# A triangular inverse by doubling: 64x64 tiles on TensorE's diagonal, or 32x32 tiles for its first four steps

## The chip, the cores and the metric

One Trainium2 chip, one of its cores. The metric is the device time of one launch in microseconds (us). One execution is also recorded by the profiler; its times are those of the tables and profile lines below. Engines go by short names: PE is TensorE's matrix multiplication and PEld its weight load, DVE is VectorE, ACT is ScalarE, POOL is GpSimd, and SP issues the DMA transfers.

## The reference

A gated delta rule over a sequence is followed by an MLP mixer, all in fp32. Batch is 4, heads 8, sequence 768, head dimension 48. Cut to what matters:

```python
k_n = k / (norm(k) + 1e-6)
for t in range(S):                                # per batch and head, state is 48 x 48
    y[t] = q[t] @ state
    v_old = state.T @ k_n[t]
    state = state + beta[t] * outer(k_n[t], v[t] - v_old)
x = y as (B, S, H * D)                            # 768 tokens of 384
h = relu(x.T @ w_tok1) @ w_tok2                   # token mixing, 768 -> 256 -> 768
u = x + h.T
out = u + relu(u @ w_ch1) @ w_ch2                 # channel mixing, 384 -> 1536 -> 384
```

## The kernel before

The sequence is cut into chunks of 128 tokens: 6 chunks for each of 4 batches, 24 in all, each with its 8 heads side by side. Within a chunk the recurrence is solved at once. With G the strictly triangular part of the beta-weighted products of the keys, the kernel needs W, the inverse of I + G, for each head (128x128). Four generators make the program:

- `prep(t)` does what doesn't depend on the state: it norms the keys (`ksq` to `krec`, `kpad`, `kbpad`), transposes (`p_t`, L301), forms the products (`p_g`, L313) and masks them on DVE into `gm` (L317). Then it builds W.
- `recur(t)` carries the state through the chunk (`p_b` L432, `p_u` L439, `p_s` L447, `p_y` L464 and L469). It uses W as `w_t`.
- `mixer(b)` is the MLP of a batch whose six chunks are done: `p_1` (L483), `p_h` (L495), transposes (L506), `p_c` (L517), `p_o` (L529).
- `load_weights` brings in the four weight matrices and rounds them with bit operations, mostly on DVE, one on POOL (L199 to L221), during the first chunks.

W is built by doubling. It begins as the identity, minus the entries of `gm` at odd columns that couple neighbours (`off`, L333 and L338 on POOL). For block sizes s = 2, 4, 8, 16, 32, one `step` joins pairs of blocks of size s into blocks of 2s. A step is a chain over two engines:

1. DVE transposes W in 32x32 blocks into T (`flip`, L345).
2. PE multiplies `gm` with the even columns of T into `p_l` (L359). This is one burst of matmuls over all heads and all tiles on the diagonal.
3. DVE masks it into `lt` (L360).
4. PE multiplies `lt` with the odd columns of W into `p_wu` (L372), again a burst.
5. DVE subtracts that from the odd columns of W (L373), called `w_o`.

In the kernel before, every step works on tiles of R = 64: rows and columns 0 to 63, and 64 to 127, so that a burst is 8 heads times 2 tiles, 16 matmuls. An fp32 matmul is two instructions of PE in the profile, each with its weight load, so a burst shows as x32. The tiles have 64 columns for each head in `w_r`, `t_r` and `lt_buf`.

After s = 32 both 64x64 diagonal blocks of W are done (`w_6`, `t_6`, which are `w_r` and `t_r` here). A correction of T (`p_x`, L399 and L400), a product (`p_l`, L410) and a last one (`p_wu`, L415) give the 64x64 block off the diagonal. POOL copies (L404 to L406) and ACT (L411, L416) fill `w_t`.

The order of the program comes from `plan`, a heap of generators with a start time and a step in units of a chunk: prep(t) runs one unit ahead of recur(t), and mixer(b) is spread over the six chunks after its batch. The framework then orders the instructions for each engine by that priority and by readiness, and places the semaphores. So matmuls of the mixer stand between the bursts of a prep where there are any. There are none for the first six chunks, apart from the first products of the mixer (L483). The last mixer stands alone at the end.

The sizes that follow R are these lines:

```python
ident_r = folded("ident_r", ident, R)
mask_1 = folded("mask_1", mask_f, R // 2)
SMALL = [s for s in (2, 4, 8, 16, 32) if s < R]
width = (R if s < R else 64) // 2          # of masks[s]
width = R if s < R else 64                 # of lt_buf[s]
for lo in range(0, 128, R):                # off, one POOL instruction for each tile
```

Of the kernel before, what the change touches and what calls it, by code (L numbers as in the profile page):

```python
# [13 lines left out]

C = 128
DP = 64
R = 64
WP = 384


# [1 line left out]
def kernel(  # L22
# [76 lines left out]
    def folded(name, full, width):  # L99

        t = const.tile([128, width], FP32, name=name)
        nc.gpsimd.tensor_copy(out=t, in_=full[:, 0:width])
        for lo in range(width, full.shape[-1], width):
            nc.gpsimd.tensor_tensor(
                out=t, in0=t, in1=full[:, lo : lo + width], op=ALU.add
            )
        return t

    ident_r = folded("ident_r", ident, R)

# [3 lines left out]
    for sign in (1, -1):  # L114
# [3 lines left out]
        )  # L118
    mask_1 = folded("mask_1", mask_f, R // 2)

    SMALL = [s for s in (2, 4, 8, 16, 32) if s < R]
    masks = {}
    for s in (2, 4, 8, 16, 32):
# [9 lines left out]
        )  # L133
        width = (R if s < R else 64) // 2
        masks[s] = folded(f"mask_{s}", m.rearrange("p n s -> p (n s)"), width)
# [11 lines left out]
    for s in (2, 4, 8, 16, 32):  # L147
        width = R if s < R else 64
        lt_buf[s] = const.tile([128, H, width], FP32, name=f"lt_{s}")
# [112 lines left out]
    def prep(t):  # L262
# [62 lines left out]

        w_r = work.tile([128, H, R], FP32, name="w_r", bufs=1)
        t_r = work.tile([128, H, R], FP32, name="t_r", bufs=1)
# [277 lines left out]
```

## Time and profile before

| | |
|---|---|
| time, median of 3 runs | 1278.59 us (1268.81 to 1278.84) |
| the profiled execution | 1278.59 us |
| its span, first to last instruction | 1276.8 us |
| granted PE clock, mean | 0.908 |
| PE busy | 1169.6 us (92%) |
| PEld busy | 920.6 us (72%) |
| DVE busy | 431.3 us (34%) |
| POOL busy | 197.0 us (15%) |
| ACT busy | 180.7 us (14%) |
| chain that ended last | PE 86%, DVE 8%, POOL 4% |

A line of the costliest groups gives the line of the kernel, the engine and the operation, what is written and read, the size (for PE rows*columns of the tile and partitions x elements of the moving operand), the count, then busy us, mean ns of one, and the idle time of that engine just before such instructions, with what ended it. A matmul is pipelined, and its end is modelled, so its mean ns is longer than the pace at which matmuls follow each other. A line of the timeline gives start and duration in us of several merged instructions, their count, and in brackets the idle time before them. The row of PEclk gives the granted clock of PE in tenths, in 40 slices of 31.9 us.

### The profile page before, as it was taken

Reading aid. Unit: us, or ns where it says so; the run is one execution under the profiler, and the core shown is the slowest. Engines: PE = TensorE matmul, PEld = TensorE weight load, DVE = VectorE, ACT = ScalarE, POOL = GpSimd, SP = SyncE. Lnnn points to the kernel's source line nnn. Section 1 sums busy time; section 2 is a strip of 40 time slices with the busy share of each in tenths; the row PEclk is TensorE's granted clock in tenths of the full one; section 3 lists DMA queues with packets and bytes.
Section 4 is the critical chain, followed back from the end, with each engine's and each line's share of the span. In section 5 each row is a group of like instructions: output and inputs, shape, how many; then the busy total and the mean of one; then the engine's idle time right before and its main releaser. Section 6 shows DMA issues by size and latency. Waiting matters only on the chain.

```text
span 1276.8 us, 27386 instructions
## 1 busy us (share of the span) xinstructions
PE 1169.6 (92%) x12462; PEld 920.6 (72%) x12462; DVE 431.3 (34%) x898; ACT 180.7 (14%) x407; POOL 197.0 (15%) x295
## 2 busy tenths in 40 slices
PE   4788787788999999999999999999999999999998
PEld 3767676677787777777677777777677777786776
DVE  6766674332334323322322313322323322211000
ACT  2001011011111120120121120220121120111111
POOL 6233141111111110110110110110111110000000
PEclk9986575776999999899897998999799999799999
DMA  6232230010001000100000100100000000000000
GB/s 123 79 85 77 70 89 25 14 26 8 15 14 26 21 13 15 32 13 14 20 14 8 32 14 14 32 14 14 20 14 8 14 1 8 7 1 13 13 13 13
DMA packets 83395, 33.31 MB, mean 26 GB/s; under 512 B 75824, under 2 KB 78896, under 8 KB 83280
## 3 DMA queue, kind: packets, MB, share of 16 engines
q1 hardware_dynamic: 83280, 31.56, 10.2%
q8 instruction: 98, 1.61, 0.5%
q14 instruction: 17, 0.14, 0.0%
HBM read 26.84 MB, written 4.72 MB: 25 GB/s over the span
## 4 chain that ended last, share of the span: by engine, by line
PE 86%; DVE 8%; POOL 4%; issue 2%; ACT 0%; POOLq 0%; ACTq 0%
PE p_c L517 15%; PE p_o L529 15%; PE p_l L359 12%; PE p_wu L372 12%; PE p_g L313 4%; PE p_u L439 4%; PE p_y L469 4%; PE p_h L495 3%; PE p_t L301 3%; PE p_l L410 2%; PE p_wu L415 2%; PE p L483 2%; DVE t_r L345 2%; PE p_x L399 2%; POOL off L333 2%
## 5 line engine op out<-in xcount | busy, mean ns | idle before, releaser
L517 PE MATMUL p_c<-u_t,wc 128*128 128x256 f32 x864 | 227.8, 405 | 0.1
L359 PEld LDWEIGHTS p_l<-t_r,gm 64*64 64x64 f32 x3840 | 144.3, 155 | 111.4 <-issue 89.4
L359 PE MATMUL p_l<-t_r,gm 64*64 64x32 f32 x3840 | 157.3, 238 | 65.0 <-DVE t_r L345 60.0
L529 PE MATMUL p_o<-wc,r 128*128 128x384 f32 x576 | 216.8, 507 | 0.0
L372 PEld LDWEIGHTS p_wu<-w_r,lt 64*64 64x64 f32 x3840 | 146.5, 158 | 56.7 <-DVE lt L360 33.0
L517 PEld LDWEIGHTS p_c<-u_t,wc 128*128 128x128 f32 x864 | 159.7, 197 | 25.5 <-issue 2.6
L372 PE MATMUL p_wu<-w_r,lt 64*64 64x32 f32 x3840 | 160.6, 240 | 14.0 <-DVE lt L360 14.0
L529 PEld LDWEIGHTS p_o<-wc,r 128*128 128x128 f32 x576 | 101.2, 191 | 50.9 <-issue 2.9
L360 DVE TENSOR_TENSOR lt<-p_l,mask 128x256 f32<-128x256 f32 x120 | 50.9, 424 | 175.2 <-PE p_l L359 175.0
L317 DVE TENSOR_TENSOR gm<-p_g,mask_u 128x512 f32<-128x512 f32 x96 | 62.0, 685 | 129.3 <-PE p_g L313 129.2
L373 DVE TENSOR_TENSOR w_r<-w_r,p_wu 128x256 f32<-128x256 f32 x120 | 50.6, 421 | 158.8 <-PE p_wu L372 158.6
L345 DVE STREAM_TRANSPOSE t_r<-w_r 128x512 f32<-128x512 f32 x120 | 85.2, 710 | 45.6 <-POOL w_r L338 43.2
L522 ACT ACTIVATE r<-p_c 128x256 f32<-128x256 f32 x144 | 55.2, 383 | 249.6 <-PE p_c L517 249.6
L405 POOL COPY w_t<-w_r 64x512 f32<-64x512 f32 x24 | 15.0, 625 | 455.0 <-DVE w_r L373 455.0
L313 PE MATMUL p_g<-kbq_t,k_t 64*128 64x256 f32 x384 | 64.3, 423 | 3.8 <-DVE gm L317 3.2
L536 DVE TENSOR_TENSOR o_sb<-p_o,xb 128x384 f32<-128x384 f32 x24 | 13.4, 557 | 135.4 <-PE p_o L529 135.4
L313 PEld LDWEIGHTS p_g<-kbq_t,k_t 64*128 64x128 f32 x384 | 41.1, 198 | 20.3 <-DVE gm L317 6.5
L411 ACT COPY lt<-p_l 64x512 f32<-64x512 f32 x24 | 13.9, 580 | 279.6 <-PE p_l L410 279.6
L469 PE MATMUL p_y<-u,gm 128*128 128x48 f32 x384 | 52.1, 289 | 0.0
L469 PEld LDWEIGHTS p_y<-u,gm 128*128 128x128 f32 x384 | 50.0, 207 | 1.9 <-issue 1.0
L333 POOL TENSOR_TENSOR off<-gm,mask 64x256 f32<-64x256 f32 x48 | 36.0, 750 | 78.0 <-DVE gm L317 76.5
L215 POOL TENSOR_TENSOR w_f<-w_f,w_r 128x384 uint32<-128x384 uint32 (+1 forms) x34 | 33.5, 986 | 91.5 <-DVE w_f L207 77.8
(89 smaller groups left out, 1076.5 us busy)
## 6 DMA issues: line engine op xcount, KB each, us to landing
d<-in_moe_w_ch_dram SPq DMA_DIRECT2D x24, 384.0 KB, 3.2
k_raw<-in_k_dram SPq DMA_DIRECT2D x24, 192.0 KB, 2.7
qpad<-in_q_dram SPq DMA_DIRECT2D x24, 192.0 KB, 2.9
v_raw<-in_v_dram SPq DMA_DIRECT2D x24, 192.0 KB, 2.6
out_dram<-o_sb SPq DMA_DIRECT2D x24, 192.0 KB, 1.9
d<-in_moe_w_tok_dram SPq DMA_DIRECT2D x6, 256.0 KB, 3.0
d<-in_moe_w_tok_dram SPq DMA_DIRECT2D x4, 384.0 KB, 3.1
beta_sb<-in_beta_dram SPq DMA_DIRECT2D x1, 96.0 KB, 2.2
```

Source lines behind the costliest of these rows:

```text
L313: nc.tensor.matmul(p_g[par][:, jj], k_t[lo : lo + DP, j], kbq_t[lo : lo + DP, j])
L317: nc.vector.tensor_tensor(out=gm[:, 4 * g + par : 4 * g + 4 : 2], in0=p_g[par], in1=mask_u[:, None, None, :].to_broadcast([128, 2, 2, 128] ...
L333: nc.gpsimd.tensor_tensor(out=off[lo : lo + R], in0=gm[lo : lo + R, :, 0, lo + 1 : lo + R : 2], in1=mask_1[lo : lo + R, None, :].to_broadc ...
L345: nc.vector.transpose(dst.rearrange("p h n -> p (h n)"), src.rearrange("p h n -> p (h n)"))
L359: nc.tensor.matmul(p_l[r, h], gm[r, h, 0, r], t_e[r, h])
L360: nc.vector.tensor_tensor(out=lt_e, in0=halves(p_l, s), in1=halves(masks[s][:, None, :], s).to_broadcast([128, H, half // s, s]), op=ALU.mult,
L372: nc.tensor.matmul(p_w[r, h], lt[r, h], w_o[r, h])
L439: nc.tensor.matmul(p_u[:, h], w_t[:, h], rhs[:, h])
L469: nc.tensor.matmul(p_y[:, h], gm[:, h, 1], u[:, h], start=(c == 0 and h == 0), stop=(h == H - 1), skip_group_check=True,)
L517: nc.tensor.matmul(p_c, wc1[:, cb, f * 128 : (f + 1) * 128], u_t[:, cb], start=(cb == 0), stop=(cb == NCB - 1),)
L522: nc.scalar.activation(r, p_c, ACTF.Relu)
L529: nc.tensor.matmul(p_o, r2[f][:, i * C : (i + 1) * C], wc2[:, f], start=(f == 0), stop=(f == NHT - 1),)
```

## The change

The constant R becomes 32:

```diff
-R = 64
+R = 32
```

All that follows from it:

- `w_r`, `t_r`, `off`, `ident_r`, the masks and `lt_buf` of the steps s = 2 to 16 are half as wide.
- The bursts of these four steps run over four tiles of 32x32 on the diagonal: 8 heads times 4 tiles, 32 matmuls with 16 moving columns each. `step(s, R, w_r, t_r)` is called with 32.
- The loop over `lo` makes four `off` instructions on 32 partitions.
- Before s = 32 this branch, not taken at R = 64, spreads W and T to 64 columns for each head. `half_of` is 1 on the partitions of the first, or of the second, 32 of each 64 rows and 0 elsewhere, so that each 32x32 block lands in its place on the diagonal of its 64x64 tile:

```python
w_6 = work.tile([128, H, 64], FP32, name="w_6", bufs=1)
t_6 = work.tile([128, H, 64], FP32, name="t_6", bufs=1)
for i in range(2):
    c_i = slice(32 * i, 32 * i + 32)
    nc.gpsimd.tensor_scalar_mul(w_6[:, :, c_i], w_r, half_of[:, i : i + 1])
    nc.gpsimd.tensor_scalar_mul(t_6[:, :, c_i], t_r, half_of[:, i : i + 1])
```

- The step s = 32 and all after it run on `w_6` and `t_6` in 64x64 tiles as before.
- T was and is made by DVE transposes of 32x32 blocks, now of 128x256 elements instead of 128x512.

## The prediction

> **What bounds the kernel now.** I read the busy shares and the 40 slices first, then the costliest groups, then the timeline of single steps.
>
> ```profile
> PE 1169.6 (92%) x12462; PEld 920.6 (72%) x12462; DVE 431.3 (34%) x898; ACT 180.7 (14%) x407; POOL 197.0 (15%) x295
> ...
> PE   4788787788999999999999999999999999999998
> ...
> PEclk9986575776999999899897998999799999799999
> ...
> L359 PE MATMUL p_l<-t_r,gm 64*64 64x32 f32 x3840 | 157.3, 238 | 65.0 <-DVE t_r L345 60.0
> L372 PE MATMUL p_wu<-w_r,lt 64*64 64x32 f32 x3840 | 160.6, 240 | 14.0 <-DVE lt L360 14.0
> ...
> L345 DVE STREAM_TRANSPOSE t_r<-w_r 128x512 f32<-128x512 f32 x120 | 85.2, 710 | 45.6 <-POOL w_r L338 43.2
> ```
>
> From slice 11 (about 320 us) on TensorE (PE) is the bound; before that it waits more and its clock is down. The doubling steps (L359 and L372) hold 318 us of modelled matmul time, so the price of one burst of theirs decides. One step early and one late, from the timeline:
>
> ```profile
> 144.83 1.92 PE L359 MATMUL p_l<-t_r,gm 64*64 64x32 f32 x32 [1.70 <-DVE t_r L345]
> 146.78 0.42 DVE L360 TENSOR_TENSOR lt<-p_l,mask 128x256 f32<-128x256 f32 x1 [0.63 <-PE p_l L359]
> 147.26 1.92 PE L372 MATMUL p_wu<-w_r,lt 64*64 64x32 f32 x32 [0.52 <-DVE lt L360]
> 149.23 0.42 DVE L373 TENSOR_TENSOR w_r<-w_r,p_wu 128x256 f32<-128x256 f32 x1 [1.02 <-PE p_wu L372]
> 150.04 0.70 DVE L345 STREAM_TRANSPOSE t_r<-w_r 128x512 f32<-128x512 f32 x1
> 150.89 1.92 PE L359 MATMUL p_l<-t_r,gm 64*64 64x32 f32 x32 [1.70 <-DVE t_r L345]
> ...
> 365.54 1.12 PE L359 MATMUL p_l<-t_r,gm 64*64 64x32 f32 x32
> 366.60 1.13 PE L517 MATMUL p_c<-u_t,wc 128*128 128x256 f32 x4
> 367.66 1.12 PE L372 MATMUL p_wu<-w_r,lt 64*64 64x32 f32 x32
> 368.71 1.56 PE L517 MATMUL p_c<-u_t,wc 128*128 128x256 f32 x6
> ```
>
> Early, a step is one bare chain of 6.06 us, 3.84 of it two bursts at half clock. Late, the mixer's matmuls fill the gaps and PE never stops: each us taken out of a burst comes off the end.
>
> **What limits a burst.** A burst is 16 matmuls, each two instructions in fp32, so 32 weight loads and 32 matmuls. Compare a burst on both 64x64 tiles with one on a single tile (8 matmuls), and two cuts of the timeline 6 ns apart:
>
> ```profile
> 633.23 1.01 PEld L359 LDWEIGHTS p_l<-t_r,gm 64*64 64x64 f32 x32 [0.55 <-issue]
> ...
> 598.57 1.00 PEld L399 LDWEIGHTS p_x<-lt,w_r 64*64 64x64 f32 x16 [0.55 <-DVE w_r L373]
> 603.01 1.00 PEld L415 LDWEIGHTS p_wu<-w_r,lt 64*64 64x64 f32 x16 [0.54 <-issue]
> 604.96 1.86 PEld L439 LDWEIGHTS p_u<-bv,w_t 128*128 128x128 f32 x16 [0.30 <-POOL w_r L328]
> ...
> 633.23 0.25 PEld L359 LDWEIGHTS p_l<-t_r,gm 64*64 64x64 f32 x5 [0.55 <-issue]
> 633.23 0.25 PEld L359 LDWEIGHTS p_l<-t_r,gm 64*64 64x64 f32 x6 [0.55 <-issue]
> ```
>
> Twice the loads in the same time: the two tiles run side by side. The cuts at 633.340 and 633.346 us hold five and six loads: the other tile's load starts 6 ns after the first's. Within one tile the loads follow at (1.00 - 0.135)/15 = 58 ns for 64 columns, the same for 32 (L399) and 64 moving columns (L415), and at (1.86 - 0.19)/15 = 111 ns for 128 columns. So the weight load sets the pace, about 53 ns per 64 columns and 5 ns fixed; 32 columns would follow at about 31 ns.
>
> The Trainium skill agrees on this much. "TensorEngine Tiling (Array Packing)", Key Properties: tiles load and multiply in parallel (the trace agrees, 32 loads against 16 in 1.0 us), and a change of tiling mode drains the array (each burst here ends about 0.07 us after the next work has begun, and the number of changes stays). "TensorE: Matmul & The Clock Gate", LDWEIGHTS: the time goes with the columns, not the rows (58 against 111 ns). Against it stands Instruction Overhead on the first page: about 60 cycles a matmul whatever its width. The trace has two matmuls 6 ns apart on different tiles, so I take this as a floor for each tile, 25 ns at 2.4 GHz, below the 31 ns. No row shows four tiles at once.
>
> **The change part by part**, for 24 chunks. Steps s = 2 to 16 change shape, s = 32 stays.
>
> 1. PE bursts, 8 a chunk, 192 in all: 32 matmuls of 32x32 with 16 moving columns instead of 16 of 64x64 with 32, so 64 loads and 64 matmuls over four tiles, 16 rounds. At 31.4 ns a round and the same 0.19 us of entry and tail (1.12 - 16 x 0.058) the burst takes 0.69 us: 0.43 saved. At half clock a round falls from 107 to about 53 ns (64 columns at half speed), 1.95 to 1.14 us: 0.80 saved. Going by burst starts in the timeline, some 13 of the 48 bursts before 317 us ran at full clock and 35 at half; of the 144 later ones some 132 and 12. Early: 13 x 0.43 + 35 x 0.80 = 33.6. Late: 132 x 0.43 + 12 x 0.80 = 66.4.
> 2. DVE, narrower: the 128x256 product takes 421 ns and the 128x384 one (rhs) 551, so 1.0 ns an element. lt and w_o at 128 elements: about 0.29, 0.13 saved, 8 a chunk. Transpose 512 to 256: 0.71 to 0.45, 0.26 saved, four visible a chunk (the fifth goes beside part 4). 2.1 us of chain a chunk; early 6 x 2.1 = 12.7, late nothing, as mixer work covers it.
> 3. POOL, first product: off becomes four instructions on 32 partitions instead of two at 750 ns. By L104 (317 ns at 64 elements) and 750 at 256, one of 128 costs 0.46: 1.85 against 1.50, +0.35. L338 halves, 0.78 to about 0.49. Sum nearly 0, +0.2 taken; early +1.3. The narrower ident copy is hidden: POOL waits for PE before it anyway.
> 4. POOL, new: four tensor_scalar_mul spread w_r and t_r into 64 columns (w_6, t_6) between the s = 16 step and the s = 32 burst, in place of an immediate start. No row shows one; bounds are 0.43 us (a one-input copy at 1.0 ns an element, from 688 ns at 512) and 0.78 (L338, 256 strided elements). I take 0.5, 2.0 in a row, the DVE flip beside the first: wait after w_o from about 0.9 to 2.2, +1.3 a chunk (range +1.0 to +2.4). Queued behind them on POOL are only the w_t copies, which have over 20 us of idle before them. Early nothing covers it: 6 x 1.3 = 7.8. Late the gap held some 1.1 to 1.6 us of mixer work, and more can be put there because the program order is laid out by readiness; I take +0.3 a chunk, +5 (uncovered: +16).
> 5. Masks and memsets at the start: some 0.1 us each beside the first loads; nothing. No DMA and no queue of SP moves.
>
> Early: -33.6 - 12.7 + 1.3 + 7.8 = -37, of which I count -33, because weight-rounding work on DVE (0.35 to 1.0 us pieces in the same queue) takes some of the openings. Late: -66.4 + 5 = -61. The last 137 us are one mixer alone and stay. The clock may give some back: PE was granted half clock when less dense, and I add 5 (an estimate without a row). Sum -89 against the profiled execution: span 1276.8 - 89 + 1.8 outside it = 1190, and that execution is also the median of the three runs (1278.59; the lowest is 1268.81).
>
> **Rivals.**
> A, the forecast: four tiles side by side, 0.69 us a burst, about 1190; own range 1160 to 1220.
> B, issue binds a little: if the 6.5 ns seen between tiles were the price of each single instruction, a round is 8 x 6.5 = 52 ns, a burst 1.02 us. 145 x 0.1 = 15 saved at full clock, at half clock 47 x 0.8 = 38 at most, -4 from the rest and the clock: 1230 to 1270, by how the half-clock bursts are fed.
> C, the other side: twice the instructions cost twice the time, because instruction supply to PE, not the array, becomes the limit. Place: each of the 192 bursts. Price: the densest sustained rate in this trace is one load and matmul in 28.9 ns; at that rate 64 pairs take 1.85 + 0.19 = 2.04 us, +0.92 on 145 bursts, +0.15 on the 47 at half clock: +141, about 1419. At the skill's 60 cycles taken for the whole array, 25 ns a matmul: 1.79 us, +97, about 1376. It decides from a burst of about 1.2 us on, 7.9 ns an instruction, as parts 2 to 4 cancel to within 4 us. For it: nothing in the trace ever ran denser, PE had bursts of at most 64 instructions queued, now 128. Against it: at the head of a burst load, matmul, load, matmul start within 7 ns, and the period halves or doubles with the clock (58 to 107 ns), which a supply limit would not do.
> That four 32x32 tiles don't overlap fully is part of C by its price.
>
> **How the numbers follow.** A 0.50, B 0.10, C 0.40. The measurement tells about 1% (13 us) from no change. A is all faster; of B 0.07 is faster and 0.03 within 1%; of C 0.04, where supply binds only little, is within 1%, and 0.36 slower. So faster 0.57, same 0.07, slower 0.36. The range runs from A's lower end to C's upper price: 1160 to 1420.
>
> **What would show it.** Right: x32 loads become x64 at L359 with the PE burst at 0.6 to 0.75 us late, and the granted clock no worse; L345 near 450 ns; L360 and L373 near 290; four new POOL rows near 0.5 us, with PE p_l of s = 32 waiting on t_6 early. Wrong: late bursts of 1.2 us or more, in which the loads of one tile are over 75 ns apart; or bursts as short as forecast and a clock below 0.85, so that the mixer slows.

## The result, and the profile after

The changed kernel takes 1361.53 us (median of 4 runs, 1342.9 to 1376.08), the kernel before 1277.38 us beside it. The ratio is 1.0625, with a 95% interval of 1.0504 to 1.0746: 6% slower. The forecast was 1190 us. The profiled execution took 1360.47 us, its span is 1358.4 us. Executions of one kernel differ by up to 6% with the clock that they were granted; medians here are of all of them, ratios leave out those more than 1.5% above the kernel's fastest.

The bursts did nearly what was forecast. The page after, with the rows that answer to those shown of before:

```profile
PE 1191.2 (88%) x18606; PEld 909.1 (67%) x18606; DVE 372.1 (27%) x898; ACT 182.2 (13%) x407; POOL 285.3 (21%) x451
...
PEclk9967556767777989776877868799798879799999
...
L359 PE MATMUL p_l<-t_r,gm 32*32 32x16 f32 x6144 | 78.5, 188 | 53.2 <-DVE t_r L345 48.3
L391 POOL TENSOR_SCALAR w<-w_r,half_of 128x256 f32<-128x256 f32 x48 | 45.4, 956 | 302.8 <-DVE w_r L373 302.8
L372 PE MATMUL p_wu<-w_r,lt 32*32 32x16 f32 x6144 | 82.4, 190 | 25.3 <-DVE lt L360 14.8
L359 PE MATMUL p_l<-t,gm 64*64 64x32 f32 x768 | 32.7, 242 | 53.9 <-POOL t L392 53.9
```

L359 and L372 held 318 us of modelled matmul time over five steps, about 254 of it in the four that change (four fifths, an estimate by count); their 32x32 bursts now hold 161 us. But one operation that spreads W and T takes 0.92 to 0.96 us instead of the estimated 0.5, PE waits 53.9 us for T alone, and the row of the clock is full of sevens and eights after slice 10, where it had nines. One s = 16 step, the wait and what comes after it, from the timeline:

```profile
416.57 0.91 PE L529 MATMUL p_o<-wc,r 128*128 128x384 f32 x2
417.41 0.72 PE L372 MATMUL p_wu<-w_r,lt 32*32 32x16 f32 x64
...
418.65 1.82 POOL L391 TENSOR_SCALAR w<-w_r,half_of 128x256 f32<-128x256 f32 x2 [13.50 <-DVE w_r L373]
420.46 1.82 POOL L392 TENSOR_SCALAR t<-t_r,half_of 128x256 f32<-128x256 f32 x2
421.43 1.12 PE L359 MATMUL p_l<-t,gm 64*64 64x32 f32 x32 [1.56 <-POOL t L392]
...
425.51 1.65 PE L529 MATMUL p_o<-wc,r 128*128 128x384 f32 x2
427.09 1.91 PE L399 MATMUL p_x<-lt,w 64*64 64x32 f32 x16
```

The 32x32 burst of 64 matmuls takes 0.72 us, against 1.12 us for 32 matmuls on 64x64 tiles. Then four POOL operations take 3.6 us, first both of W, then both of T. The next burst starts 0.05 us after the third of them, as it reads the first 32 columns of T alone; before that PE is idle for 1.56 us. After that the same two matmuls of the mixer take 1.65 us instead of 0.91. The stretches of the trace around it show why; the columns are stretch, length, busy us and count of PE, PEld, DVE, ACT and POOL, granted clock, DMA share and GB/s:

```profile
404.50:419.80 15.30, 15.08 (x544) 9.46 (x542) 5.82 (x17) 1.40 (x4) 1.80 (x3) 1.00 0.06 14
419.80:423.00 3.20, 1.64 (x35) 1.31 (x34) 0.40 (x1) 0.00 (x0) 3.20 (x5) 0.99 0.02 5
423.00:437.00 14.00, 14.00 (x91) 9.18 (x90) 1.42 (x4) 0.58 (x1) 1.63 (x3) 0.52 0.11 29
```

In the third stretch PE is busy throughout, at half speed. The clock did not go down in the wait but 1.5 us after its end, at 422.9 us, and stayed down for 13.7 us of full PE work.

By stages, from the masked products of chunk 6 to the last product of the last W: early, up to chunk 6, 313.3 us before and 301.3 after, 12 won; late 823.6 and 916.8, 93 lost; the last mixer alone 140 in both.

### The profile page after: what moved, and what is told of

The parts are those of the page before. It is cut to its first block, busy times and chain, and to the rows that moved or that the text cites. A ratio compares the mean times of both kernels' runs of the same rounds, so it can differ in the third digit from the quotient of the medians.

```text
span 1358.4 us, 39863 instructions
## 1 busy us (share of the span) xinstructions
PE 1191.2 (88%) x18606; PEld 909.1 (67%) x18606; DVE 372.1 (27%) x898; ACT 182.2 (13%) x407; POOL 285.3 (21%) x451
## 4 chain that ended last, share of the span: by engine, by line
PE 77%; POOL 9%; DVE 9%; issue 4%; DMA 1%; ACT 1%; POOLq 0%; DVEq 0%; ACTq 0%; SPq 0%
PE p_o L529 15%; PE p_c L517 15%; PE p_wu L372 8%; PE p_l L359 7%; PE p_u L439 4%; PE p_g L313 4%; PE p_y L469 3%; PE p_t L301 3%; PE p_l L410 3%; PE p_wu L415 3%; POOL off L333 3%; PE p_h L495 3%; PE p_x L399 3%; POOL w L391 2%; PE p L483 2%
## 5 line engine op out<-in xcount | busy, mean ns | idle before, releaser
L359 PEld LDWEIGHTS p_l<-t_r,gm 32*32 32x32 f32 x6144 | 69.4, 116 | 91.7 <-issue 71.3
L359 PE MATMUL p_l<-t_r,gm 32*32 32x16 f32 x6144 | 78.5, 188 | 53.2 <-DVE t_r L345 48.3
L372 PEld LDWEIGHTS p_wu<-w_r,lt 32*32 32x32 f32 x6144 | 71.5, 119 | 62.8 <-issue 31.0
L391 POOL TENSOR_SCALAR w<-w_r,half_of 128x256 f32<-128x256 f32 x48 | 45.4, 956 | 302.8 <-DVE w_r L373 302.8
L372 PE MATMUL p_wu<-w_r,lt 32*32 32x16 f32 x6144 | 82.4, 190 | 25.3 <-DVE lt L360 14.8
L360 DVE TENSOR_TENSOR lt<-p_l,mask 128x128 f32<-128x128 f32 (+1 forms) x120 | 38.0, 316 | 198.8 <-PE p_l L359 197.9
L359 PE MATMUL p_l<-t,gm 64*64 64x32 f32 x768 | 32.7, 242 | 53.9 <-POOL t L392 53.9
L359 PEld LDWEIGHTS p_l<-t,gm 64*64 64x64 f32 x768 | 29.9, 160 | 64.7 <-POOL t L392 64.7
L313 PE MATMUL p_g<-kbq_t,k_t 64*128 64x256 f32 x384 | 68.6, 446 | 3.5 <-DVE gm L317 2.7
L345 DVE STREAM_TRANSPOSE t_r<-w_r 128x256 f32<-128x256 f32 x120 | 53.3, 444 | 53.4 <-POOL w_r L338 50.6
L333 POOL TENSOR_TENSOR off<-gm,mask 32x128 f32<-32x128 f32 x96 | 45.4, 472 | 95.1 <-DVE gm L317 90.7
L313 PEld LDWEIGHTS p_g<-kbq_t,k_t 64*128 64x128 f32 x384 | 43.1, 208 | 21.8 <-DVE gm L317 7.3
```

Source lines behind the costliest of these rows:

```text
L313: nc.tensor.matmul(p_g[par][:, jj], k_t[lo : lo + DP, j], kbq_t[lo : lo + DP, j])
L333: nc.gpsimd.tensor_tensor(out=off[lo : lo + R], in0=gm[lo : lo + R, :, 0, lo + 1 : lo + R : 2], in1=mask_1[lo : lo + R, None, :].to_broadc ...
L345: nc.vector.transpose(dst.rearrange("p h n -> p (h n)"), src.rearrange("p h n -> p (h n)"))
L359: nc.tensor.matmul(p_l[r, h], gm[r, h, 0, r], t_e[r, h])
L372: nc.tensor.matmul(p_w[r, h], lt[r, h], w_o[r, h])
L391: nc.gpsimd.tensor_scalar_mul(w_6[:, :, c_i], w_r, half_of[:, i : i + 1])
```

## The experiments

The theory: the POOL wait opens a gap on PE; with short bursts beside it, too little array work is left, the clock is halved, and mixer work pays for it. Rivals: 32x32 tiles bring the clock down whatever the waits; or the waits are lost time by themselves and the clock matters little. For each kernel the table gives the median time and, from its profiled execution, the granted clock from 317 us to the end, and the half-clock time in it, added up from the clock record of the trace (it is about 2 x (1 - clock) x length).

| kernel | time, us | profiled execution, us | clock after 317 us | half clock there, us | late stage, us |
|---|---|---|---|---|---|
| before, R = 64 | 1277.4 | 1278.6 | 0.96 | 69 | 823.6 |
| changed, R = 32 | 1361.5 | 1360.5 | 0.85 | 306 | 916.8 |
| R = 32, spread on DVE and ACT | 1223.5 | 1245.2 | 0.94 | 115 | 802.9 |
| R = 64, the POOL wait added | 1346.1 | 1346.5 | 0.94 | 125 | 863.6 |
| R = 32, t_6 first in the program | 1347.6 | 1351.0 | 0.86 | 283 | 906.9 |
| R = 64, the wait, half the heads | 1275.7 | 1262.2 | 0.90 | 193 | 840.5 |
| R = 32, gap filled | 1271.8 | 1270.2 | 0.95 | 89 | 827.2 |
| R = 32, both waits cut | 1182.9 | 1173.7 | 0.99 | 12 | 744.4 |
| R = 32, POOL products | 1254.8 | 1254.8 | 0.95 | 97 | 811.7 |
| R = 64, first wait cut | 1232.5 | 1232.4 | 0.99 | 27 | 788.0 |

### The wait taken away

```diff
-                nc.gpsimd.tensor_scalar_mul(w_6[:, :, c_i], w_r, half_of[:, i : i + 1])
-                nc.gpsimd.tensor_scalar_mul(t_6[:, :, c_i], t_r, half_of[:, i : i + 1])
+                nc.vector.tensor_scalar_mul(t_6[:, :, c_i], t_r, half_of[:, i : i + 1])
+                nc.scalar.activation(
+                    w_6[:, :, c_i], w_r, ACTF.Copy, scale=half_of[:, i : i + 1]
+                )
```

> The changed kernel (R = 32) with the four spreading operations taken off POOL: t_6 by two DVE operations, w_6 by two ACT operations beside them. Theory 1 (the POOL wait of 3.7 us before the s = 32 burst opens a gap on PE, after which the clock is halved for 7 to 34 us, and the mixer pays): wait down to about 1.1 us, the gap before L359 at s = 32 gone late, half-clock time after 317 us from 306 back to about 70 us, bursts still 0.73 us, time about 1190 us (1170 to 1220). Rival (32x32 bursts keep too little of the array busy, so the clock falls whatever the waits): half-clock time after 317 us stays over 200 us, time 1290 to 1340 us.

Measured: 1223.47 us, ratio 0.958 (0.9518 to 0.9641). The spread, from the timeline:

```profile
630.34 0.91 ACT L392 ACTIVATE w<-w_r,half_of 128x256 f32<-128x256 f32 x2 [13.26 <-DVE w_r L373]
...
631.24 0.75 DVE L391 TENSOR_SCALAR t<-t_r,half_of 128x256 f32<-128x256 f32 x2
...
631.95 1.12 PE L359 MATMUL p_l<-t,gm 64*64 64x32 f32 x32
```

PE no longer waits there (no idle time before the last line). The median is 138 us below that of the changed kernel; between the two profiled executions it is 115 us, 114 of them in the late stage. The median lies just above the theory's interval and clear of the rival's. As the profiled execution took 22 us more than the median, its 115 us of half clock are rather high.

### The wait alone, on 64x64 tiles

```diff
         if R == 64:
-            w_6, t_6 = w_r, t_r
+            w_6 = work.tile([128, H, 64], FP32, name="w_6", bufs=1)
+            t_6 = work.tile([128, H, 64], FP32, name="t_6", bufs=1)
+            for i in range(2):
+                c_i = slice(32 * i, 32 * i + 32)
+                nc.gpsimd.tensor_scalar_mul(w_6[:, :, c_i], w_r[:, :, c_i], one)
+                nc.gpsimd.tensor_scalar_mul(t_6[:, :, c_i], t_r[:, :, c_i], one)
```

> The kernel before (R = 64) with only the wait added: w_6 and t_6 are made from w_r and t_r by four POOL multiplications by one, of 128x256 elements each, in the place where the changed kernel spreads. Theory 1 (wait and clock): a gap of about 1.6 us on PE before the s = 32 burst, half-clock time after 317 us up from 69 to 250 us or more, time 1400 to 1450 us, as the bursts keep their 1.12 us. Rival (32x32 bursts throttle the clock): half-clock time below 120 us, only the gaps are added, 24 x 1.5 to 3 us, time 1310 to 1345 us.

Measured: 1346.07 us, ratio 1.0541 (1.0474 to 1.0608). The waits of PE between 340 and 1120 us, in this kernel first, then in the changed one (us in total, times, longest):

```profile
PE p_l L361 <- POOL t L392: 22.2, 16, 1.6
PE p_l L361 <- DVE t_r L347: 21.0, 14, 1.8
...
PE p_l L359 <- POOL t L392: 25.8, 15, 2.1
PE p_l L359 <- DVE t_r L345: 19.3, 12, 1.8
```

In both kernels the burst starts 2.95 us after `w_o` ends (medians), against 0.95 us in the kernel before. PE covers a little more of that here: 22.2/16 = 1.4 us idle a time, against 25.8/15 = 1.7. The late clock is 0.94, not 0.85. My theory of a gap that brings the clock down by itself fell here: half-clock time after 317 us is 125 us, half of what I had forecast and close to the rival's bound of 120. Of the 125 us, 49 end a stretch that began at 301.5 us, in the early stage; a later expectation counts 76 us without them. The time is at the rival's upper edge. Early, where there is no mixer work to fill anything, the half-clock time did rise, from 167 to 225 us, and the stage from 313.3 to 341.7 us.

The four times together give a sum: the wait costs 69 us on 64x64 tiles (1346.1 - 1277.4), 40 of them in the late stage, and 138 us on 32x32 tiles (1361.5 - 1223.5), 114 of them in the late stage. The tiles win 54 us without the wait and lose 15 with it. So in these four kernels most of the loss goes with the two together; what differs between them in the trace is told under "What the windows show".

### Half the wait

```diff
+            for i in range(2):
+                c_i = slice(32 * i, 32 * i + 32)
+                nc.gpsimd.tensor_scalar_mul(t_6[:, :, c_i], t_r, half_of[:, i : i + 1])
             for i in range(2):
                 c_i = slice(32 * i, 32 * i + 32)
                 nc.gpsimd.tensor_scalar_mul(w_6[:, :, c_i], w_r, half_of[:, i : i + 1])
-                nc.gpsimd.tensor_scalar_mul(t_6[:, :, c_i], t_r, half_of[:, i : i + 1])
```

> The changed kernel with the two t_6 multiplications put ahead of the two of w_6 on POOL. The s = 32 burst needs t_6 alone, so its wait falls from 3.7 to about 2.4 us (flip 0.45, two at 0.92), while w_6 is ready some 1.8 us later, by the time the second product needs it. Theory 1 (wait and clock): the gap shrinks to at most 0.5 us late or goes, half-clock time after 317 us falls well below 306, to between 70 and 200 us, time 1210 to 1290 us. Rival (32x32 bursts throttle): only the gap itself is won, some 1 us a chunk, time 1325 to 1350 us.

Measured: 1347.62 us, ratio to before 1.0539 (1.0449 to 1.0628). That is the rival's figure, but the edit did not do what it was meant to do. From the timeline of this kernel, where L394 makes `w_6` and L391 makes `t_6`:

```profile
575.63 1.82 POOL L394 TENSOR_SCALAR w<-w_r,half_of 128x256 f32<-128x256 f32 x2 [12.39 <-DVE w_r L373]
...
577.43 1.82 POOL L391 TENSOR_SCALAR t<-t_r,half_of 128x256 f32<-128x256 f32 x2
...
578.40 1.12 PE L359 MATMUL p_l<-t,gm 64*64 64x32 f32 x32 [1.78 <-POOL t L391]
```

The framework orders the instructions of an engine by readiness too, and POOL still does both operations of `w_6` first, in all 24 chunks, as in the changed kernel. The wait after `w_o` is 2.95 us in both. So the run says nothing of a shorter wait. It is a second measurement of the changed kernel, 14 us (1%) below the first.

### Short bursts without 32x32 tiles

```diff
+            hs = H if s == 32 else H // 2
...
-            for h in range(H):
+            for h in range(hs):
...
-            flip(t_r, w_r)
+            flip(t_r[:, : H // 2], w_r[:, : H // 2])
```

> R = 64 with the POOL wait of the earlier run, and the steps s = 2 to 16 done for heads 0 to 3 alone (the other four heads are left out of them): 8 matmuls on two 64x64 tiles a burst, some 0.65 us, DVE operations of the same element counts as at R = 32. So the durations are those of the changed kernel, without a 32x32 tile. Theory 1 (what counts is how much array work falls into a window of the clock control, so short bursts and a gap together bring it down, whatever the tile): half-clock time after 317 us up from 76 to 200 us or more, time 1330 to 1400 us. Rival (the 32x32 shape itself brings the clock down): half-clock time stays below 120 us, and the time falls by the shorter bursts, to 1260 to 1295 us.

Measured: 1275.68 us (median of 20 runs, 1234.72 to 1282.61, 15 of them from 1274 to 1283). The time is the rival's, the clock is nearly the theory's. The stretch from 317 us on, with the wait and whole bursts, and with the wait and half bursts:

```profile
317.00:1345.00 1028.00, 969.86 (x9900) 738.69 (x9900) 258.99 (x514) 150.19 (x346) 176.71 (x235) 0.94 0.06 14
317.00:1260.00 943.00, 895.88 (x7126) 660.27 (x7124) 207.00 (x485) 142.15 (x330) 163.53 (x217) 0.90 0.06 15
```

Half-clock time goes from 125 to 193 us (from 100 to 207 us in the late stage) with no 32x32 tile in the kernel. So the clock comes down without that tile shape. Whether it is the short bursts that bring it down is not shown by this; more on it under "What the windows show". My time was too high because I started from the changed kernel and not from 1346 us less 24 x 8 bursts of some 0.45 us. It is still 86 us faster than the changed kernel with 113 us less half-clock time, so this run does not give the whole of the changed kernel's loss; what the tile shape adds stays open.

### The gap filled with useless work

```diff
+        p_d = ps_att([128, H * R], "p_d")
+        for i in range(4):
+            nc.tensor.matmul(p_d, ident, w_r.rearrange("p h n -> p (h n)"))
         yield from step(32, 64, w_6, t_6)
```

> The changed kernel with four matmuls of no use (identity by w_r, 128x128 with 256 moving columns, result unread) put between the s = 16 step and the s = 32 burst, where PE waits for POOL. They add 24 x 1.7 = 41 us of PE work at full clock. Theory 1 (array work in a window sets the clock): the gap fills, half-clock time after 317 us falls from 306 to below 180 us, and the time falls in spite of the added work, to 1290 to 1345 us. Rival (the waits are the loss, the clock only goes with them or with the tile shape): no gain, 1365 to 1405 us.

Measured: 1271.8 us, ratio to before 0.9981 (0.9947 to 1.0015). Adding work to PE made the changed kernel 90 us faster, more than I expected. The waits of PE between 340 and 1120 us:

```profile
PE p_l L359 <- DVE t_r L345: 23.9, 14, 1.8
PE p_l L359 <- POOL t L392: 7.8, 12, 0.7
```

The wait for POOL is still there, but only 0.7 us at most is idle. Half-clock time after 317 us falls from 306 to 89 us. The POOL operations were not touched, nor were the tiles: it is the missing array work in the gap that costs.

### Both waits cut

```diff
         for lo in range(0, 128, R):
-            nc.gpsimd.tensor_tensor(
+            eng = nc.gpsimd if lo < 64 else nc.vector
+            eng.tensor_tensor(
                 out=off[...], ...
-        nc.gpsimd.tensor_tensor(
+        nc.vector.tensor_tensor(
             out=w_r[:, :, 1::2], in0=w_r[:, :, 1::2], in1=off, op=ALU.subtract
```

This is added to the version with the spread on DVE and ACT.

> The changed kernel with the spread on DVE and ACT as before, and the other POOL wait cut too: two of the four off products and the subtraction after them go to DVE, so that the chain from the mask to the first transpose falls by about 1.1 us. Theory 1: the gap of 1.75 us before the first burst of a chunk falls to about 0.7 us, half-clock time after 317 us falls below 80 us, time 1180 to 1210 us. Rival (these gaps are harmless, as the kernel before has them at full clock): 1205 to 1225 us, the 24 x 0.3 us or less that is no longer waited for.

Measured: 1182.9 us, ratio 0.9262 (0.9182 to 0.9343), the fastest of all. In the changed kernel, and in this one, from 317 us on, and this kernel's waits of PE between 340 and 1120 us:

```profile
317.00:1358.00 1041.00, 970.98 (x13925) 719.48 (x13924) 207.67 (x494) 146.41 (x337) 166.60 (x258) 0.85 0.06 14
...
317.00:1172.00 855.00, 831.08 (x13723) 622.02 (x13719) 231.34 (x572) 160.26 (x369) 80.02 (x134) 0.99 0.07 17
...
PE p_l L360 <- DVE t_r L346: 8.9, 15, 0.7
```

The gap before the first burst of a chunk falls from 1.8 to at most 0.7 us, and the late clock is full but for 12 us.

The same cut of the first wait on 64x64 tiles, by the same diff on the kernel before:

> The kernel before (R = 64) with the off products halved between POOL and DVE and the subtraction after them on DVE, as in the fastest R = 32 version, so that the two differ by the tiles and the spread alone. Theory 1 (at R = 64 a window holds enough array work beside a gap of 1.75 us, so the gap costs its own length and little clock): the gap falls by about 1.2 us a chunk, time 1235 to 1262 us, and the tiles' own worth is the rest, 55 to 75 us. Rival (the cut gap is what made the fast version fast, at either tile size): 1180 to 1215 us.

Measured: 1232.51 us, ratio 0.9651 (0.9607 to 0.9696), 2.5 us below what the theory gave. So the cut alone is worth 45 us at R = 64, and 41 us at R = 32 (1223.5 - 1182.9). For this wait the tile size made no difference, and at R = 64 too the clock had its part in it: half-clock time fell from 69 to 27 us. The tiles with the fast spread are worth another 50 us (1232.5 - 1182.9).

### The price of the POOL form

```diff
-                nc.gpsimd.tensor_scalar_mul(w_6[:, :, c_i], w_r, half_of[:, i : i + 1])
-                nc.gpsimd.tensor_scalar_mul(t_6[:, :, c_i], t_r, half_of[:, i : i + 1])
+                for dst, src in ((w_6, w_r), (t_6, t_r)):
+                    nc.gpsimd.tensor_tensor(
+                        out=dst[:, :, c_i], in0=src,
+                        in1=half_of[:, i : i + 1, None].to_broadcast([128, H, R]),
+                        op=ALU.mult,
+                    )
```

> The changed kernel with the four POOL operations written as products of two tensors, the second one a broadcast of half_of, instead of a tensor by a scalar for each partition. Theory: the 0.92 us of one is the price of the scalar form, not of 256 strided elements, so a product takes about 0.78 us as L338 did with 256 elements. Rival: the strided target is what costs, 0.9 us or more. The time moves little either way, 1330 to 1370 us.

Measured in one run: 1254.76 us. The groups, and the wait of PE from 340 to 1120 us:

```profile
L392 POOL TENSOR_TENSOR w<-w_r,half_of 128x256 f32<-128x256 f32 x48 | 29.5, 635 | 305.6 <-DVE w_r L373 305.6
...
PE p_l L359 <- POOL t L392: 13.0, 16, 1.1
```

One operation takes 0.64 us, so it was the scalar form that cost 0.92. The burst now starts 1.95 us after `w_o`, 1.0 us sooner than in the changed kernel. That is 24 us over the chunks, and the time moved by 107 us. Half-clock time fell from 306 to 97 us, 209 us less, which is enough for the rest. I had said that the time would hardly move.

### What the windows show

The Trainium skill, "TensorE: Matmul & The Clock Gate", Part 1 (The HAM clock gate), says that the clock is set by the array's activity in windows of about 3.4 us that run freely, and that one idle window halves it. The trace agrees on the window: in all ten kernels the changes of the clock fall on a grid of 3.4133 us, within 2 ns. It does not agree that a window must be idle. I added up, for each window after 320 us, the matmuls' streaming time times the share of the 128 rows that their tile has. Streaming takes about 0.83 ns a moving column at full clock ((1.56 - 1.13)/2 us for 256 columns in the late `p_c` lines of the prediction) and twice that at half clock. The 123 windows at full clock that were followed by half clock held 0.18 to 0.39 of a full window in the ten kernels; the 2280 followed by full clock held 0.37 or more. A line at 0.37 sorts all but 6 of them; without the weight by rows the best line leaves 78 on the wrong side. From half back to full it took 0.67 or more, in 104 of 126 windows 0.75 or more, while windows that stayed at half held up to 0.79. So PE need not be idle for the clock to fall; a window with about three eighths of the rows' work is on the edge. This sum was made after the runs and fits them; no run was made to place the threshold.

The falls can be put down to pauses of PE as well. For each fall after 320 us I took the longest pause in the window before it. "The first wait" is that of the first burst of a chunk; waits count here that start at full clock and leave PE idle for over 0.3 us.

| kernel | falls at the POOL wait | half clock after them, us | falls at the first wait | half clock after them, us |
|---|---|---|---|---|
| before, R = 64 | no such wait | 0 | 6 of 15 | 68 |
| changed, R = 32 | 10 of 17 | 188 | 10 of 16 | 72 |
| R = 32, spread on DVE and ACT | no such wait | 0 | 12 of 16 | 89 |
| R = 64, the POOL wait added | 1 of 18 | 14 | 9 of 15 | 61 |
| R = 64, the wait, half the heads | 7 of 15 | 113 | 5 of 15 | 78 |
| R = 32, t_6 first in the program | 10 of 17 | 191 | 10 of 16 | 61 |
| R = 32, gap filled | 0 of 13 | 0 | 14 of 17 | 85 |
| R = 32, both waits cut | no such wait | 0 | 0 of 16 | 0 |
| R = 32, POOL products | 1 of 17 | 10 | 9 of 17 | 58 |
| R = 64, first wait cut | no such wait | 0 | 3 of 11 | 24 |

So 188 of the 237 us of half clock that the change added (306 - 69) follow the POOL wait, and 44 follow three pauses inside bursts (last section). Where that wait is filled, or leaves PE idle for 0.8 us (POOL products), the clock falls there once or never. In the changed kernel a fall at the POOL wait lasts 4 to 10 windows, one at the first wait 1 to 4. It fits that the steps after the POOL wait (s = 32, L399, L410, L415, on one or two 64x64 tiles) hardly fill a window to three quarters.

Why the POOL wait alone did so little on 64x64 tiles is open. The smaller work of the short bursts is not the direct reason: in the windows that hold the pause the bursts of s = 2 to 16 make up only about 0.01, in either kernel. Two things do differ. The pause is shorter there, 1.4 us against 1.8. And it lies differently: in the kernel with the wait added to 64x64 tiles, 16 of 19 pauses began 1.9 to 3.1 us into a window of 3.41 us, so that two windows shared them. All ten pauses with a fall in the changed kernel, and all seven in the one with half the heads, began within 1.0 us after the start of a window or within 0.6 us before it. With half the heads the pause is the shortest of the three, 1.25 us, and the clock falls all the same. No run varied length and place of the pause apart.

## Why the prediction was wrong

- **What limits a burst, and part 1, right.** 0.69 us at full clock were forecast, 0.72 to 0.73 were measured in nine bursts of ten, and 1.05 at half clock (1.14 forecast). Loads of the four tiles run side by side: 64 of them in 0.63 us. (58 against 111 ns, which the prediction gives for the columns, changed rows and columns together. The trace of the kernel before has the case apart: the median load of 64 rows and 128 columns, L313, lasts 187 ns, of 128 and 128 192, L439, and of 64 and 64 135, L359.)

```profile
417.41 0.63 PEld L372 LDWEIGHTS p_wu<-w_r,lt 32*32 32x32 f32 x64 [0.55 <-DVE lt L360]
```

- **Rival C, wrong in its mechanism, right in its sign.** Instruction supply does not set the pace of a burst. The measured time lies 15 us below C's lower price all the same, for another reason. That it lies in the range of 1160 to 1420 us is luck: that end of the range was C's.
- **Part 2, right.** Transposes 444 ns (0.45 forecast), the narrow lt 289 and w_o 287 ns (0.29).
- **Part 3, right.** An off product takes 472 ns (0.46), L338 482 (0.49).
- **Part 4, the size was wrong.** One spreading operation takes 0.92 us; I took 0.5 and bounded it by 0.78. Four take 3.7 us instead of 2.0. PE needs three of them, so the wait after `w_o` became 2.95 us instead of 2.2; this is 2.0 more than before, inside the range of +1.0 to +2.4. The bound came from rows of other forms, and a form without a row can lie above all of them.
- **Part 4, the cover was wrong as well.** I held that mixer work would be put into the wait, at 0.3 us a chunk. The gap was 1.56 us in the example, 25.8 us over 15 waits in the middle of the kernel: 1.7 us each.
- **The clock is the step that failed most.** I added 5 us for it, without a row. It took 237 us more of half clock after 317 us (306 - 69). If PE had been busy all along, that is a loss of half, 118 us. The 90 us that came back when the gap was filled, with work added, bear this size out. I named the clock under what would make the prediction wrong, but gave it no chance and no price of its own.
- **The early stage** won 12 us where I counted 33. The POOL wait does not account for it: with the spread on DVE and ACT the stage is only 0.7 us shorter, 300.6 us, at 191 us of half clock instead of 178. The difference was not traced.
- **The sum for 1190 us** was within reach of the tiles themselves: with both waits cut, R = 32 takes 1182.9 us. But 41 us of that come from a cut that wins 45 us at R = 64 as well.

## What to carry to other kernels

A stage's speed is also the clock it leaves for the next one: before a change shortens TensorE's work or adds a wait beside it, add up how much array work is left in each window of 3.4 us around the gaps, at the kernel's own tile sizes. The same wait for POOL cost 69 us over 24 chunks in the kernel with long bursts and 138 us in the one with short ones, and filling it with useless matmuls won 90 us. In these traces how much of a pause lay in one window mattered, and not its length alone. After a change of order in the program, read in the trace whether the engine follows it. Price a new operation from a row of the same form, or measure it first: here the scalar form on POOL took 0.92 us and the product form 0.64.

## What the runs showed that I had not expected

- Four 32x32 tiles on the diagonal take a load and a matmul every 8 ns at full clock ((0.63 - 0.11) us over 63 steps, as one load lasts 0.11 us), more than three times the densest rate in the kernel before.
- Bursts on 32x32 tiles sometimes stop in the middle for no wait that the profile shows. In the changed kernel 12 such stops leave PE idle for over 0.3 us, 11 us together; one of them:

```profile
673.00 0.71 PE L372 MATMUL p_wu<-w_r,lt 32*32 32x16 f32 x63
675.01 0.20 PE L372 MATMUL p_wu<-w_r,lt 32*32 32x16 f32 x1 [1.30 <-issue]
```

  The six kernels with R = 32 have 5 to 12 of them, the four with R = 64 none. Late supply of instructions would look like this; it was not tested.
